# Seven octets in the first chunks' absorb, GpSimd's adds for seven pairs, and octet six's copies on another queue

## The chip, the cores and the metric

The kernel runs on one core of one Trainium2 chip. The metric is the device time of one execution in microseconds (us), as the median of several runs. A profiled execution gives the trace; its times are counted from the start of the span, that is, from the first to the last instruction of the core.

## What is computed

The reference, cut to what matters: linear attention with a feature map of two exponentials, then a Fourier mix of the sequence axis, then a channel product with a relu.

```python
def _attn_ref(q, k, v, w_phi):                    # 8 batches, 8 heads, 576 tokens, 64 wide
    def phi(x):
        proj = np.einsum('bhsd,df->bhsf', x, w_phi)
        proj = proj - np.max(np.abs(proj), axis=-1, keepdims=True)
        return np.concatenate([np.exp(proj), np.exp(-proj)], axis=-1)
    q_p, k_p = (phi(q), phi(k))
    kv = np.einsum('bhsf,bhsd->bhfd', k_p, v)
    z = np.sum(k_p, axis=2)
    num = np.einsum('bhsf,bhfd->bhsd', q_p, kv)
    den = np.einsum('bhsf,bhf->bhs', q_p, z)[..., None] + 1e-06
    return (num / den).astype(np.float32)

def _moe_ref(x, w_r, w_i, w_ch):                  # x: 8 x 576 x 512, the heads side by side
    X = np.fft.rfft(x, axis=1)
    Y = np.zeros_like(X)
    Xr, Xi = (np.real(X[:, :n_modes]), np.imag(X[:, :n_modes]))       # 64 modes
    Yr = np.einsum('bmd,mde->bme', Xr, w_r) - np.einsum('bmd,mde->bme', Xi, w_i)
    Yi = np.einsum('bmd,mde->bme', Xr, w_i) + np.einsum('bmd,mde->bme', Xi, w_r)
    Y[:, :n_modes] = Yr + 1j * Yi
    y = np.fft.irfft(Y, n=S, axis=1)
    u = x + y
    return (u + np.maximum(u @ w_ch, 0.0)).astype(np.float32)
```

## The kernel before

The tokens of a pair of batches (`bp`, 0 to 3) lie in nine chunks (`n`, 0 to 8) of 128 rows: chunk n below 8 holds 128 tokens of one of the two batches, chunk 8 the last 64 of both. The result x of the attention stays in SBUF in bf16, as tile `xs`; `chunk(bp, n)` is its view of one chunk, 128 x 512. The rows of a chunk are in another order than the output wants them, except those of chunk 8: a matmul with the permutation `perm` on the left, in place of the identity `ident_b`, brings them into the stored order.

The first stage (16 units of a group of heads `g` and a pair `bp`) computes the attention and x's first 64 Fourier modes. The mode weights, 64 MB in float32 that pass as bf16 in 1 MB pieces, are loaded by GpSimd's queue (`wload`) throughout the whole run, in the order of the list `order`; tiles of tag `wt` (pool `pw`, eight slots) hold them. The modes are worked off in eight octets `o`. `mix(g, w, ...)` multiplies one piece. Of the list the last eight pieces belong to octets six and seven.

Behind the attention the loop over `mixq` does a `mix`, then some items of the list `todo` (`fill`). In `todo` stand:

- `hold(i)` for each of the 36 chunks: `Channels.turn` transposes the chunk on TensorE (PE) and VectorE (DVE) copies it out as `xT`; `Channels.product` multiplies it by w_ch and ScalarE (ACT) keeps the result in `xw`. Each `hold` first takes a step of the generator `inverse_tables`, which builds the inverse Fourier tables `CI`, `CL`, `CM` on VectorE, with tile `xw` of the last pair as its scratch.
- an `Absorb` for each chunk: `sum_p` adds y's first octets to x, `sum_q` adds y @ w_ch to `xw`, by the identity and by matmuls with `CI` on the left (`back`). Before the change 96 rows, that is octets 0 to 5, take part. VectorE adds x (`keep_x`), ACT keeps `xw` (`keep_w`).

When an octet is complete, its sum `yst` (y) is transposed and multiplied by w_ch, which gives `zst`. `put` copies both by DMA: octets 0 to 5 into the rows of `yall` and `zall` that `Absorb` reads, octets 6 and 7 each four times into `yl`, at the rows that `late` reads.

When the last octet is there, the pairs of chunks in `seq` are finished (class `Last`), 20 items, four of them single chunks. `base(1)` opens a PSUM bank with the permuted `xw` (q), `base(0)` one with the permuted x (p); `late` adds octets 6 and 7 from `yl` with `CL` on the left, q with `late(1)`, p with `late(0)`. For the four chunks with bp = 0 and n below 4 (`early`) `late` adds octet 6 alone and `straight` adds octet 7 straight from `yst` and `zst` with `CM`. `relu` is ACT's relu of q into `rl`; `store` is VectorE's p + rl into `of` (tag `wt`) and the DMA to the output. The banks q come from pool `pst` (four banks), the banks p from `pst2` (two tiles of two banks). The loop at the end prepares q of the next item while it finishes p of the present one:

```python
    for g, s in enumerate(seq):
        t = seq[g + 1] if 0 < g < len(seq) - 1 else None
```

All engines take their instructions in the order in which they are written down (`InOrder`), so an instruction that waits holds up all behind it on its engine. The helper that does this is line 37, which is why most rows of the trace carry L37; they are told apart by their tiles.

Of the kernel before, what the change touches and what calls it, by code (L numbers as in the profile page):

```python
# [20 lines left out]
NG = 4  # L21
# [22 lines left out]
def kernel(  # L44
# [534 lines left out]
    CL = pb.tile([128, 5, 128], BF16, name="CL", bufs=1)  # L579
    perm = CF.rearrange("p c t x m -> p (c t x m)")[:, 512:640]  # L580
# [5 lines left out]
    def inverse_tables():  # L586
# [37 lines left out]
        for dst, m, r, only in ((CI, mode, r, None), (CL, late, r, None), (CM, last, rm, b0)):  # L624
# [17 lines left out]
            if dst is CI:  # L642
                dve.tensor_scalar_mul(out=dst.rearrange("p c s -> p (c s)"), in0=rnd[:, :n],
                                      scalar1=amp)
                yield
                continue
# [9 lines left out]
    class Channels:  # L656
# [4 lines left out]
        def turn(self):  # L661
# [5 lines left out]
            dve.tensor_copy(self.xT, pt)  # L667
# [13 lines left out]
    def back(p, c, bp, table, src, r, stop=True):  # L681

        if c < 8:
            pe.matmul(p, lhsT=table[r, c % 4, :], rhs=src[r, 2 * bp + c // 4, :],
                      start=(src is yall), stop=stop)
        else:
            for i in range(2):
                pe.matmul(p[64 * i:64 * i + 64, :], lhsT=table[r, 4, 0:64],
                          rhs=src[r, 2 * bp + i, :], start=(src is yall), stop=True)

    class Absorb:

        def __init__(self, bp, n):
            self.bp, self.n = bp, n

        def sum_p(self, p):
            self.p = p
            back(p, self.n, self.bp, CI, yall, slice(0, 96))

        def sum_q(self, q):  # L700
            self.q = q
            pe.matmul(q, lhsT=ident_b, rhs=xw[:, self.bp, self.n, :], start=True, stop=False)
            back(q, self.n, self.bp, CI, zall, slice(0, 96))
# [13 lines left out]
        def only_w(self):  # L717
            back(self.q, self.n, self.bp, CI, zall, slice(0, 96))
            self.keep_w()

        def all(self):
            if chunks.index((self.bp, self.n)) % 2:
# [9 lines left out]
    chunks = [(bp, n) for bp in range(NP) for n in range(9)]  # L732
    ch = [Channels(*c) for c in chunks]
    ab = [Absorb(*c) for c in chunks]
    K = len(ch) - 3

    tables = inverse_tables()

    def hold(i):
# [3 lines left out]
        if i < K:  # L743
            ch[i].product()
            return
# [8 lines left out]
    todo += [c.only_x for c in ab[K:]] + [c.only_w for c in ab[K:]] + [c.all for c in ab[:K]]  # L754
# [7 lines left out]
    def put(src, o, dst, copies):  # L762
        if o < 6:
            sp.dma_start(dst[16 * o:16 * o + 16], src)
        else:
            for s in copies:
                r = 32 * s + 16 * (o - 6)
                (sp, pool)[s // 2 if o == 7 else 0].dma_start(yl[r:r + 16], src)


    class Last:

        def __init__(self, *items):
# [3 lines left out]
            self.first = bp == 0 and n < 2  # L777

        def base(self, which):
# [9 lines left out]
            for a, (bp, n) in enumerate(self.items):  # L789
                turned = perm if n < 8 else ident_b  # L790
# [7 lines left out]
        def late(self, which):  # L798
            for a, (bp, n) in enumerate(self.items):
                r = 64 * a + 32 * which  # L800
                back((self.q if which else self.p)[a], n, bp, CL, yl,
                     slice(r, r + 16 if self.early else r + 32), not self.early)
# [11 lines left out]
        def relu(self):  # L814
            self.rl = pb.tile([128, 2, DMODEL], F32, name="rl")
            for a in range(len(self.items)):
                act.activation(self.rl[:, a], self.q[a], ACT.Relu)

# [25 lines left out]
    seq = [Last((0, 0)), Last((0, 1))] + [Last(*x) for x in pairs[0][1:] + pairs[1]]  # L844
    seq += [Last((0, 8), (1, 8))] + [Last(*x) for x in pairs[2]] + [Last((2, 8), (3, 8))]
# [116 lines left out]
```

## Time and profile before

| | us |
|---|---|
| median of 8 runs | 444.65 (443.95 to 445.76) |
| profiled execution | 445.15 |
| its span | 443.2 |
| busy: PE, VectorE, ScalarE, GpSimd | 337.5, 284.2, 279.5, 84.5 |
| mean granted TensorE clock | 0.90 |

A row of the trace gives an instruction's start and duration, the engine, the operation, what it writes and reads with partitions x elements, and how many were merged (x4). In brackets, or behind a bar, stands the engine's idle time before it and what ended it. The end of a matmul is modelled, so two in a row are best told by their starts: 0.217 us from one dense 512-column matmul to the next at full clock. A weight load is PEld, GpSimd is POOL, SyncE's DMA queue is SP.

### The profile page before, as it was taken

Reading aid. Unit: us, or ns where it says so; the run is one execution under the profiler, and the core shown is the slowest. Engines: PE = TensorE matmul, PEld = TensorE weight load, DVE = VectorE, ACT = ScalarE, POOL = GpSimd, SP = SyncE. Lnnn points to the kernel's source line nnn. Section 1 sums busy time; section 2 is a strip of 40 time slices with the busy share of each in tenths; the row PEclk is TensorE's granted clock in tenths of the full one; section 3 lists DMA queues with packets and bytes.
Section 4 is the critical chain, followed back from the end, with each engine's and each line's share of the span. In section 5 each row is a group of like instructions: output and inputs, shape, how many; then the busy total and the mean of one; then the engine's idle time right before and its main releaser. Section 6 shows DMA issues by size and latency. Waiting matters only on the chain.

```text
span 443.2 us, 10464 instructions
## 1 busy us (share of the span) xinstructions
PE 337.5 (76%) x4389; PEld 217.8 (49%) x4433; DVE 284.2 (64%) x561; ACT 279.5 (63%) x488; POOL 84.5 (19%) x126
## 2 busy tenths in 40 slices
PE   3577668677686685785976777876899859999994
PEld 2356547545475573664754655652455424343231
DVE  4667586555865757867668568658744323776685
ACT  4588687666976866867778659433444312665673
POOL 7132122122221211321232021140011110000000
PEclk9969887689988969988889789698899978999998
DMA  8999999999999999999999999999999999993697
GB/s 174 235 211 211 238 212 237 238 212 263 211 213 236 238 236 237 210 238 211 239 220 226 237 212 239 209 213 212 212 224 222 218 219 219 211 220 64 214 383 287
DMA packets 51487, 99.31 MB, mean 224 GB/s; under 512 B 2480, under 2 KB 13616, under 8 KB 51440
## 3 DMA queue, kind: packets, MB, share of 16 engines
q0 software_dynamic: 45280, 86.19, 99.0%
q1 hardware_dynamic: 6160, 12.45, 8.0%
q8 instruction: 34, 0.56, 0.5%
q14 instruction: 13, 0.11, 0.1%
HBM read 163.64 MB, written 9.44 MB: 391 GB/s over the span
## 4 chain that ended last, share of the span: by engine, by line
issue 33%; PE 25%; DMA 13%; ACT 11%; DVE 8%; POOL 8%; POOLq 0%; ACTq 0%; DVEq 0%
DMA wt<-in_moe_w_i_dram 13%; PE pt L37 8%; PE one L37 7%; PE pp L37 5%; PE two L37 5%; POOL wt L37 4%; ACT AB L37 4%; DVE m L37 3%; ACT AQ L37 2%; DVE mk L37 2%; DVE xs L37 1%; ACT XT L37 1%; POOL qb L37 1%; ACT qT L37 1%; POOL kb L37 1%
## 5 line engine op out<-in xcount | busy, mean ns | idle before, releaser
L37 ACT ACTIVATE AB<-two 128x1024 bf16<-128x1024 f32 x64 | 62.1, 1028 | 12.0 <-DVE mk L37 8.6
L37 ACT ACTIVATE AQ<-two 128x1024 bf16<-128x1024 f32 x64 | 62.7, 1047 | 3.5 <-PE two L37 3.4
L37 ACT CAST xw<-pt 128x512 bf16<-128x512 f32 x50 | 29.4, 587 | 40.8 <-PE pt L37 40.7
L37 DVE TENSOR_REDUCE mk<-two 128x8 f32<-128x1024 f32 x32 | 38.9, 1218 | 14.5 <-PE two L37 14.5
L37 DVE TENSOR_REDUCE m<-two 128x8 f32<-128x1024 f32 x32 | 39.2, 1224 | 12.8 <-PE two L37 12.6
L37 DVE RECIPROCAL rd<-one 128x6 f32<-128x6 f32 x48 | 9.4, 195 | 55.9 <-PE one L37 55.8
L37 DVE TENSOR_TENSOR va<-vn,ee 128x1152 bf16<-128x1152 f32 x32 | 41.9, 1353 | 0.0
L37 PE MATMUL pt<-wchb,xT 128*128 128x512 bf16 x128 | 36.4, 399 | 6.0 <-DVE xT L37 4.5
L37 ACT COPY kT<-one 128x512 bf16<-128x512 bf16 (+1 forms) x32 | 19.3, 640 | 31.0 <-PE one L37 30.9
L37 PEld LDWEIGHTS <-xs 128*128 128x128 bf16 x624 | 31.9, 103 | 12.9 <-issue 7.0
L37 PEld LDWEIGHTS <-minus 96*128 96x128 bf16 x288 | 28.0, 116 | 17.7 <-issue 12.5
L37 PE MATMUL two<-w2blk,qT 128*128 128x256 bf16 x128 | 20.9, 289 | 19.1 <-ACT AB L37 9.2
L37 POOL DMA_DIRECT2D wt<-in_moe_w_r_dram x30 | 22.3, 744 | 68.5 <-PE one L37 34.8
L37 POOL DMA_DIRECT2D wt<-in_moe_w_i_dram x28 | 20.9, 746 | 74.3 <-PE one L37 39.8
L37 PE MATMUL two<-mT,minus 96*128 96x128 bf16 x256 | 30.8, 255 | 3.7 <-issue 2.5
L37 PEld LDWEIGHTS <-qT 128*128 128x128 bf16 x144 | 14.3, 102 | 36.6 <-issue 33.9
L37 PE MATMUL one<-wt,XT 128*32 128x512 bf16 x304 | 26.6, 436 | 5.9 <-DVE XT L37 2.7
L37 PE MATMUL one<-kvz,AQ 128*128 128x65 bf16 x512 | 29.5, 217 | 0.0
L37 PEld LDWEIGHTS <-XT 128*32 128x32 bf16 x512 | 14.5, 149 | 27.9 <-issue 13.7
L37 DVE TENSOR_TENSOR xs<-one,rd 128x384 bf16<-128x384 f32 x48 | 26.7, 557 | 1.6
L37 PEld LDWEIGHTS <-AQ 128*128 128x128 bf16 x512 | 26.5, 115 | 1.4 <-issue 0.4
L37 PE MATMUL two<-w2blk,kT 128*128 128x256 bf16 x128 | 21.1, 293 | 7.8 <-ACT AB L37 7.8
(131 smaller groups left out, 687.4 us busy)
## 6 DMA issues: line engine op xcount, KB each, us to landing
wt<-in_moe_w_r_dram POOLq DMA_DIRECT2D x30, 1024.0 KB, 21.8
wt<-in_moe_w_i_dram POOLq DMA_DIRECT2D x28, 1024.0 KB, 22.4
vn<-in_v_dram POOLq DMA_DIRECT2D x15, 576.0 KB, 17.9
out_dram<-of SPq DMA_DIRECT2D x16, 512.0 KB, 3.1
kb<-in_k_dram POOLq DMA_DIRECT2D x16, 288.0 KB, 15.4
qb<-in_q_dram POOLq DMA_DIRECT2D x16, 288.0 KB, 15.5
xs<-in_moe_w_i_dram POOLq DMA_DIRECT2D x2, 1024.0 KB, 24.2
yacc<-in_moe_w_r_dram POOLq DMA_DIRECT2D x1, 1024.0 KB, 9.6
```

Source lines behind the costliest of these rows:

```text
L37: ins = f(*args, **kwargs)
```

## The change

- `CD` is a second inverse table, `CI` with its columns in stored order, in a step of its own in `inverse_tables`. Ten chunks are `stored` and stand first in `chunks`. For these `turn` writes `xT` in stored order and `back_x` transposes it back and ACT copies it over the chunk, so that x and `xw` of these chunks are in stored order from there on.
- `Absorb` of the early chunks takes 112 rows, that is octet 6 too, and stands last (`full`); `put` copies octet 6 into `yall` and `zall` as well. `late` of early chunks falls away.
- The ten stored chunks (five pairs) and the two pairs of chunk 8 are `later`: `base(0)` does nothing for them, `late(0)` opens the bank, and GpSimd adds x to the relu's output (a tile `rx` of tag `wt`).
- `seq` takes the two pairs of chunk 8 at other places, and `ahead` says for each item which q to prepare in its step. A `later` item is prepared two or three steps before its store.
- `put` issues octet 6's copies to `yl` from GpSimd's queue, octet 7's from SP and, for the last, ACT.

```diff
--- before.py
+++ after.py
@@ -577,6 +577,8 @@
     yl = pw.tile([128, B_, DMODEL], BF16, name="yl", tag="wt")
     CI = pb.tile([128, 5, 128], BF16, name="CI", bufs=1)
     CL = pb.tile([128, 5, 128], BF16, name="CL", bufs=1)
+    CD = pb.tile([128, 4, 128], BF16, name="CD", bufs=1)
+    stored = [(1, 0), (1, 1), (1, 4), (1, 5), (2, 0), (2, 1), (2, 6), (2, 7), (3, 4), (3, 5)]
     perm = CF.rearrange("p c t x m -> p (c t x m)")[:, 512:640]
     dve.tensor_copy(perm.rearrange("k (p a) -> k a p", a=2),
                     ident_b.rearrange("k (a p) -> k a p", a=2))
@@ -643,6 +645,11 @@
                 dve.tensor_scalar_mul(out=dst.rearrange("p c s -> p (c s)"), in0=rnd[:, :n],
                                       scalar1=amp)
                 yield
+                for a in range(2):
+                    dve.tensor_copy(
+                        CD.rearrange("k c (p a) -> k a c p", a=2)[:, a],
+                        CI[:, 0:4].rearrange("k c (a p) -> k a c p", a=2)[:, a])
+                yield
                 continue
             for c in range(4):
                 dve.tensor_scalar_mul(
@@ -664,7 +671,17 @@
             for g in range(NG):
                 pe.transpose(pt[:, g, :], x[:, g, :], ident_b)
             self.xT = pb.tile([128, 4, 128], BF16, name="xT")
-            dve.tensor_copy(self.xT, pt)
+            if (self.bp, self.n) in stored:
+                dve.tensor_copy(self.xT.rearrange("p g (k a) -> p g a k", a=2),
+                                pt.rearrange("p g (a k) -> p g a k", a=2))
+            else:
+                dve.tensor_copy(self.xT, pt)
+
+        def back_x(self):
+            px = bank([128, 4, 128], BF16)
+            for g in range(NG):
+                pe.transpose(px[:, g, :], self.xT[:, g, :], ident_b)
+            act.copy(chunk(self.bp, self.n), px)
 
         def product(self):
             pf = bank()
@@ -678,29 +695,32 @@
                 pe.matmul(pf, lhsT=self.xT[:, g, :], rhs=wchb[:, g, :],
                           start=(g == 0), stop=False)
 
-    def back(p, c, bp, table, src, r, stop=True):
+    def back(p, c, bp, table, src, r, stop=True, start=False):
 
         if c < 8:
             pe.matmul(p, lhsT=table[r, c % 4, :], rhs=src[r, 2 * bp + c // 4, :],
-                      start=(src is yall), stop=stop)
+                      start=start or src is yall, stop=stop)
         else:
             for i in range(2):
                 pe.matmul(p[64 * i:64 * i + 64, :], lhsT=table[r, 4, 0:64],
-                          rhs=src[r, 2 * bp + i, :], start=(src is yall), stop=True)
+                          rhs=src[r, 2 * bp + i, :], start=start or src is yall, stop=stop)
 
     class Absorb:
 
         def __init__(self, bp, n):
             self.bp, self.n = bp, n
+            self.table = CD if (bp, n) in stored else CI
+            self.early = bp == 0 and n < 4
+            self.rows = slice(0, 112 if self.early else 96)
 
         def sum_p(self, p):
             self.p = p
-            back(p, self.n, self.bp, CI, yall, slice(0, 96))
+            back(p, self.n, self.bp, self.table, yall, self.rows)
 
         def sum_q(self, q):
             self.q = q
             pe.matmul(q, lhsT=ident_b, rhs=xw[:, self.bp, self.n, :], start=True, stop=False)
-            back(q, self.n, self.bp, CI, zall, slice(0, 96))
+            back(q, self.n, self.bp, self.table, zall, self.rows)
 
         def keep_x(self):
             x = chunk(self.bp, self.n)
@@ -715,11 +735,11 @@
             self.keep_x()
 
         def only_w(self):
-            back(self.q, self.n, self.bp, CI, zall, slice(0, 96))
+            back(self.q, self.n, self.bp, self.table, zall, self.rows)
             self.keep_w()
 
         def all(self):
-            if chunks.index((self.bp, self.n)) % 2:
+            if full.index(self) % 2:
                 p, q = bank(), bank()
             else:
                 t = banks()
@@ -730,9 +750,11 @@
             self.keep_w()
 
     chunks = [(bp, n) for bp in range(NP) for n in range(9)]
+    chunks.sort(key=lambda c: c not in stored)
     ch = [Channels(*c) for c in chunks]
     ab = [Absorb(*c) for c in chunks]
     K = len(ch) - 3
+    full = sorted(ab[:K], key=lambda c: c.early)
 
     tables = inverse_tables()
 
@@ -742,6 +764,8 @@
             ch[i + 1].turn()
         if i < K:
             ch[i].product()
+            if chunks[i] in stored:
+                ch[i].back_x()
             return
         if i == K:
             t = banks()
@@ -751,7 +775,7 @@
         ch[i].hold(ab[i].q)
 
     todo = [ch[0].turn] + [lambda i=i: hold(i) for i in range(len(ch))]
-    todo += [c.only_x for c in ab[K:]] + [c.only_w for c in ab[K:]] + [c.all for c in ab[:K]]
+    todo += [c.only_x for c in ab[K:]] + [c.only_w for c in ab[K:]] + [c.all for c in full]
     A = 3 * 3 + K
 
     def fill(n):
@@ -760,12 +784,12 @@
                 todo.pop(0)()
 
     def put(src, o, dst, copies):
-        if o < 6:
+        if o < 7:
             sp.dma_start(dst[16 * o:16 * o + 16], src)
-        else:
+        if o > 5:
             for s in copies:
                 r = 32 * s + 16 * (o - 6)
-                (sp, pool)[s // 2 if o == 7 else 0].dma_start(yl[r:r + 16], src)
+                (pool if o == 6 else act if s == 3 else sp).dma_start(yl[r:r + 16], src)
 
 
     class Last:
@@ -775,6 +799,7 @@
             bp, n = items[0]
             self.early = bp == 0 and n < 4
             self.first = bp == 0 and n < 2
+            self.later = n == 8 or items[0] in stored
 
         def base(self, which):
             if self.first:
@@ -787,7 +812,9 @@
                 self.pp = banks()
                 self.p = [self.pp[:, a] for a in range(2)]
             for a, (bp, n) in enumerate(self.items):
-                turned = perm if n < 8 else ident_b
+                turned = ident_b if self.later else perm
+                if self.later and not which:
+                    continue
                 if which:
                     pe.matmul(self.q[a], lhsT=turned, rhs=xw[:, bp, n, :],
                               start=True, stop=False)
@@ -796,10 +823,12 @@
                               rhs=chunk(bp, n), start=True, stop=False)
 
         def late(self, which):
+            if self.early:
+                return
             for a, (bp, n) in enumerate(self.items):
                 r = 64 * a + 32 * which
                 back((self.q if which else self.p)[a], n, bp, CL, yl,
-                     slice(r, r + 16 if self.early else r + 32), not self.early)
+                     slice(r, r + 32), True, self.later and not which)
 
         def straight(self, which):
             if self.early:
@@ -812,9 +841,16 @@
             act.copy(self.rl[:, 0], self.p[0])
 
         def relu(self):
-            self.rl = pb.tile([128, 2, DMODEL], F32, name="rl")
+            if self.later:
+                self.rl = pw.tile([128, 2, DMODEL], F32, name="rx", tag="wt")
+            else:
+                self.rl = pb.tile([128, 2, DMODEL], F32, name="rl")
             for a in range(len(self.items)):
                 act.activation(self.rl[:, a], self.q[a], ACT.Relu)
+            if self.later:
+                for a, c in enumerate(self.items):
+                    x = self.rl[:, a].rearrange("p (g e) -> p g e", g=4)
+                    pool.tensor_tensor(out=x, in0=x, in1=chunk(*c), op=ALU.add)
 
         def store(self):
             (bp, n), w = self.items[0], len(self.items)
@@ -841,9 +877,10 @@
                 o.rearrange("p a e -> p (a e)") if w > 1 else o)
 
     pairs = [[((bp, n), (bp, n + 1)) for n in (0, 2, 4, 6)] for bp in range(NP)]
-    seq = [Last((0, 0)), Last((0, 1))] + [Last(*x) for x in pairs[0][1:] + pairs[1]]
-    seq += [Last((0, 8), (1, 8))] + [Last(*x) for x in pairs[2]] + [Last((2, 8), (3, 8))]
+    seq = [Last((0, 0)), Last((0, 1))] + [Last(*x) for x in pairs[0][1:] + pairs[1] + pairs[2]]
     seq += [Last(*x) for x in pairs[3][:3]] + [Last((3, 6)), Last((3, 7))]
+    seq.insert(11, Last((0, 8), (1, 8)))
+    seq.insert(15, Last((2, 8), (3, 8)))
     H = DMODEL // 2
     while mixq:
         key = mixq.pop(0)
@@ -911,23 +948,30 @@
     seq[1].straight(0)
     seq[1].straight(1)
     seq[1].relu()
+    ahead = {1: [2], 2: [3], 3: [4, 5], 4: [7], 5: [6], 6: [9], 7: [8], 8: [11], 9: [10], 10: [13],
+             11: [12], 12: [15], 13: [14], 14: [17], 15: [16], 16: [18], 17: [19], 18: []}
     for g, s in enumerate(seq):
-        t = seq[g + 1] if 0 < g < len(seq) - 1 else None
-        if t and g > 1:
-            t.base(1)
-        if g > 1:
+        ts = [seq[i] for i in ahead.get(g, [])]
+        if ts and g not in (1, 3):
+            ts[0].base(1)
+        if g > 1 and g != 3:
             s.base(0)
-            if g == 2:
-                s.late(0)
-                s.straight(0)
-        if t:
+        if g == 2:
+            s.straight(0)
+            seq[4].base(1)
+            seq[3].base(0)
+        for t in ts[:1]:
             t.late(1)
         if g > 2:
             s.late(0)
-        if t:
+        for t in ts[:1]:
             t.straight(1)
             t.relu()
         s.store()
+        for t in ts[1:]:
+            t.base(1)
+            t.late(1)
+            t.relu()
     pb_cm.__exit__(None, None, None)
     pw_cm.__exit__(None, None, None)
```

## The prediction

> **What bounds the kernel now.** I read the page first (PE busy 76% of the span, DMA busy in nearly every slice up to 400 us), then busy time by stretches, then the instructions in order of time, then the groups after 411 us. All times are us from the span's start.
>
> ```profile
> 362.00:366.00 4.00, 3.12 (x19) 1.41 (x19) 1.04 (x3) 0.37 (x1) 0.74 (x1) 0.50 1.13 213
> 394.00:406.40 12.40, 12.19 (x67) 4.48 (x66) 9.71 (x15) 8.10 (x15) 0.00 (x0) 1.00 0.71 126
> 406.40:411.30 4.90, 4.84 (x33) 2.14 (x34) 2.16 (x5) 1.59 (x4) 1.10 (x2) 1.00 0.22 54
> 411.30:416.20 4.90, 4.47 (x24) 1.32 (x23) 1.93 (x3) 2.79 (x6) 0.00 (x0) 1.00 0.65 171
> 416.20:438.30 22.10, 20.77 (x124) 6.29 (x122) 19.56 (x17) 16.22 (x30) 0.00 (x0) 1.00 0.89 359
> ```
>
> The columns are length, then busy time of PE, weight load, DVE, ACT and POOL, the granted clock, DMA share and GB/s. Up to 362 the weight stream leads (213 GB/s, DMA share over 1). From 362 to the last `mix` at 406.4 PE has hardly a gap: it works off the 33 `Absorb`s, and no wait for a weight is left. From 416 to 438 three engines run level: PE, VectorE and the output at 359 GB/s, which in 420 to 422 reached 406 GB/s, so 512 KB in 1.29 us. POOL does nothing there.
>
> ```profile
> 307.56 1.89 PE L37 MATMUL pt<-wchb,xT 128*128 128x512 bf16 x4 [2.13 <-DVE xT L37]
> 350.66 0.66 PE L37 MATMUL pt<-wt,XT 128*32 128x512 bf16 x8 [1.45 <-DMA wt<-in_moe_w_i_dram]
> 362.16 1.08 PE L37 MATMUL pt<-wt,XT 128*32 128x512 bf16 x8 [3.21 <-DMA wt<-in_moe_w_i_dram]
> 405.43 0.38 PE L37 MATMUL pp<-yl,CL 16*128 16x512 bf16 x1
> 406.38 0.66 PE L37 MATMUL pt<-wt,XT 128*32 128x512 bf16 x8
> 413.68 1.23 DVE L37 TENSOR_TENSOR of<-pp,rl 128x1024 f32<-128x1024 f32 x1 [1.32 <-PE pp L37]
> 416.19 6.39 DVE L37 TENSOR_TENSOR of<-pp,rl 128x1024 f32<-128x1024 f32 x5 [1.28 <-PE pp L37]
> 437.55 0.69 DVE L37 TENSOR_TENSOR ofr<-pp,rl 128x512 f32<-128x512 f32 x1 [0.24 <-ACT rl L37]
> ```
>
> In brackets stands the wait before the row. PE waits 1.45, then 0.92 (at 356.01), then 3.21 us for weights: 5.6 us of slack before its backlog begins. After 3.21 us idle, and after 2.13, the next matmuls take twice as long (1.08 against 0.66, 1.89 against 1.03); after 1.45 they don't. The last `zst` half is ready at 410.02 (call it Z). The final sums on VectorE run to 438.24, which is Z+28.22; the span ends 4.96 us later.
>
> ```profile
> L37 DVE TENSOR_TENSOR of<-pp,rl 128x1024 f32<-128x1024 f32 x16 | 19.5, 1225 | 4.8 <-PE pp L37 4.1
> L37 PE MATMUL pp<-xs,CF 128*128 128x512 bf16 x30 | 9.1, 379 | 0.5 <-DVE of L37 0.4
> ```
>
> Of VectorE's 4.8 us of waiting between pairs PE causes 4.1. Five `of` in 6.39 us are 1.28 each, the pace to reach.
>
> **Part 1: early chunks absorb octet six.** Their eight `late` matmuls go. Four stand between 405.12 and 406.38 (base, late, base, late, each 0.31 because the row tile changes): 1.26 us. Two bases alone are 2 x 0.217 (a dense matmul's spacing) and 0.1 for the switch to the mix, so the last `mix` starts 0.73 earlier. It has room: its weight was issued at 370.37 and took 34.5, so landed at 404.9, and without part 3's copies in its way earlier still. What follows from the mix to Z is a latency chain (yst, turn, product, zst) that stays: **Z' = 409.29**. The longer absorb (112 rows for 96) costs nothing on PE, as 96 and 128 rows both show 0.38; the four absorbs come last, after 401, and octet six's zst copies of before landed at about 399.
>
> **Part 2: seven pairs take x from GpSimd.** It removes 14 `base(0)` matmuls, 14 x 0.217 = 3.0 us of PE. A step of 1.30 (two bases of 0.43, lates 0.43) becomes 0.87 at every second pair, so PE falls to 1.08 a pair on average and VectorE's 1.28 would set the pace. It adds three costs.
>
> (a) *POOL's adds.* Fourteen 128x512 adds that no row of before shows. The nearest rows:
>
> ```profile
> masks.py:199 POOL TENSOR_SCALAR_AFFINE_SELECT xs<-xs 128x128 f32<-128x128 f32 x1 | 0.3, 292 | 0.1
> masks.py:197 POOL MEMSET xs<- 128x128 f32 x1 | 0.2, 198 | 0.0
> L946 POOL MEMSET const-float32-1.0<- 128x1 f32 x1 | 0.1, 99 | 0.0
> ```
>
> Fixed cost 0.10; writing 0.77 ns an element ((198-99)/127); reading one input 0.73 more ((292-198)/128). One input at 512 elements would be 0.87 us, my lower end; a second input that costs as much as all of the first (1.5 ns) gives 1.64, my upper end. I take one more read stream, 0.10 + 512 x 2.23 ns = 1.24 us, the sum nearest to what the add does; with 0.05 between instructions 1.29. (The Trainium skill, GPSIMD Engine Reference, sections 3.1 and 4.1, advises against elementwise adds here, about twice VectorE's time: 4497 ns for 2048 elements. That would be an estimated 1.12 us, and by it the tail below would end about 0.4 us sooner.)
>
> (b) *The new order*, followed from Z'. seq[2] no longer waits for two late groups (0.32 and 0.42 in the trace): its store starts at Z'+2.7 instead of Z+3.66. seq[3] needs the octet-seven copies, issued at Z' with 3.4 to land (the SP row's median; POOL's second copy was issued 0.54 later and landed at Z+4.27): late at Z'+3.7, two relus of 0.55, store at Z'+5.1 to 6.35 (before: Z+6.17). seq[4]: `base(1)` of seq[7] is queued on PE ahead of `base(0)` of seq[4], and needs the PSUM banks that seq[4]'s relus free at Z'+6.16; then 0.43 + 0.43 + 0.43 and 0.4 of latency: store at Z'+7.7 to 8.95, a new gap of 1.3 us on VectorE. seq[5]: its relus are third in line on ACT (first half done Z'+6.7), so the adds run 6.75 to 9.3 and the store follows at 9.3.
>
> (c) From there POOL is the longest queue: 6.75 + 14 x 1.29 = 24.8, then `of` of seq[17] (0.05 + 1.24) and two single stores (0.73 each): **Z'+27.55**. VectorE alone, 1.28 x 13 + 1.46 after seq[4], would end at 27.1, so POOL costs 0.45. ACT (1.09 a pair) is hidden under both. The output, 1.29 a pair at 406 GB/s against 1.28, ends up some 0.2 later behind VectorE than now.
>
> Tail: 409.29 + 27.55 = 436.84 against 438.24, -1.4; with the output's 0.2, **-1.2 us**.
>
> (d) *Before 365.* Ten `back_x`: 4 transposes each, 0.23 us of PE (the spacing from turn to product), so 2.3 us; ten more ACT copies of 0.58 (ACT is under half busy). Ten strided xT copies and two for CD on VectorE, bounded by the dense row (0.42, no extra) and the permuting CF row:
>
> ```profile
> L37 DVE COPY xT<-pt 128x512 bf16<-128x512 bf16 x36 | 15.1, 420 | 13.3 <-PE pt L37 13.3
> L37 DVE COPY CF<-ident_b 128x128 bf16<-128x128 bf16 x1 | 0.3, 313 | 0.0
> ```
>
> A permuting copy pays (0.313-0.16)/128 = 1.2 ns an element, so up to 0.77 for 512: 3.5 us for ten, and some 0.9 for CD. VectorE is 90% busy there (10.81 of 12 us in 299 to 311) and PE waits for it, so PE falls behind by 2 to 6 us; I take 4. The 5.6 us of slack cover it; without that cover it would be paid in full. The wait at 362 then shrinks from 3.21 to 3.21 + 2.37 - 4 = 1.6 us, between the 1.45 that left the clock alone and the 2.13 that halved it. The half clock costs 2.2 us in 362 to 367 (rows 1.08, 0.72, 1.89, 0.63, 1.59 against 0.66, 0.58, 1.04, 0.38, 1.03). So this term lies between 0 and **-2.2**, and PE's backlog carries it to the end; I take -0.8. If PE falls behind by over 8 us the sign turns. (The Trainium skill, TensorE: Matmul & The Clock Gate, Part 1, puts the throttle at an idle window of about 3.4 us. The 2.13 row speaks against so sharp a bound; by the page the whole 2.2 would be won.)
>
> **Part 3: copies.** Octet six's four yl copies move from SP to POOL's queue, behind the last weights: POOL has nothing queued but the adds, and they are needed only at Z'+3.5. Two yall and zall copies come to SP. Net 0.25 MB less beside the weights (1.2 us at 213 GB/s), which hides behind PE's backlog. ACT issues one octet-seven copy; the 0.55 us of a SP issue fits before its relu at Z'+0.9. Nothing.
>
> **Sum.** Against the profiled execution (445.15, span 443.2, 1.95 around it): -1.2 - 0.8 = -2.0. The median of the runs shown is 444.65, 0.5 lower; taking the difference from it: **442.65 us**.
>
> **Rivals.** *POOL becomes the bound, and it is slower than before.* Each 0.1 us on an add is 14 x 0.1 = 1.4 us at the end. The tail's gain is gone at an add of (28.95 - 0.2 - 2.75 - 6.75)/14 - 0.05 = 1.32; with part (d) at 1.38. At 1.47 the time is 444.65 + 1.2 = 445.9 with (d), 446.7 without; at 1.64 448.2. For it: the second input shares whatever reads the first, and the seven pairs leave it only 2 x 1.28 per turn. Against: the memset and select rows. *It does not do what it says*: the gaps at seq[3] and seq[4] and slots of `wt` (rx joins `of` and yl in eight, and an `of` is free only 4.5 us after it starts) eat the tail's gain, and the clock dips as before: 444.4. *The holds overrun*: PE falls behind by over 8 us: up to 446. *Everything fits*: adds at 0.87 (-0.5) and no dip (-1.4 more): 440.7.
>
> **Numbers.** About 0.2% (0.9 us) is what a measurement of this kernel tells from no change. The forecast, with its better case, 0.62, all faster; no effect 0.12; POOL-bound 0.20 and holds overrun 0.06, slower. Range 440.7 (everything fits) to 446.6 (an add of 1.47 without the clock's help), leaving out the slower POOL adds.
>
> **What would show it.** POOL rows in the tail: fourteen adds near 1.24 us, the store of a `later` pair ending its wait on POOL. Gaps on VectorE before the stores of seq[3] and seq[4] only. The wait before the mix near 362 under 2 us and its matmuls at 0.66. Last mix about 0.7 (2 with the clock) earlier than 406.38. If the adds are over 1.33 us, or the wait for the weight near 362 is still 3 us, I am wrong in that term.

## The result, and the profile after

The changed kernel takes **443.02 us** (median of 11 runs, 441.81 to 443.88), against 444.68 us (31 runs, 443.78 to 445.76) for the kernel before in the same session. The ratio is 0.9962, 95% interval 0.9951 to 0.9972: 1.66 us less, where 2.0 were forecast (442.65).

The profiled execution took 442.19 us (span 440.3), the one of before 445.15 (443.2). The two differ by 2.96, the medians by 1.66: the profile of after caught one of its quicker executions and that of before one slower than its median. The traces serve for the order of events; what a part is worth is read from medians.

First the timeline of PE and the chain of waits of after, around the points of the prediction.

```profile
362.10 0.66 PE L37 MATMUL pt<-wt,XT 128*32 128x512 bf16 x8
...
403.76 0.66 PE L37 MATMUL pt<-wt,XT 128*32 128x512 bf16 x8
```

```profile
367.94 0.28 issue
368.22 35.49 DMA wt<-in_moe_w_i_dram
403.76 0.68 PE pt L37 x8
```

At 362 PE no longer waits, and its matmuls take 0.66 where they took 1.08: PE has fallen behind by the whole 5.6 us of slack, not by 4. The last `mix` starts at 403.76, 2.62 earlier than before (406.38). The second fence says why not earlier still: the chain that ended last goes from that `mix` to the transfer of its weight, issued at 368.22 and landed at 403.71. Before, the weight had landed at 404.9 and PE came 1.5 later; now PE and the weight arrive together.

That the weight itself lands 1.2 earlier goes with the copies: part 3 takes four from beside it and part 1 brings two. POOL did issue the load 2.15 earlier (368.22 for 370.37: a `mix` frees a slot of `wt`, and there was no half clock before it), but over the runs below the landing does not follow the issue. It follows the number of small copies of octet six that SP's queue moves beside the last weights: with none (e9, e5) the last weight lands at 402.6 and 403.0, with two (after and the eight kernels that keep its copies) at 403.2 to 404.5, with four (e1, before) at 404.6 and 404.9, with six (e2) at 405.9. The two ends of this row, from the DMA view of e9, where the load was issued at 370.21, and of e2, where it was issued at 368.02 (the last number is the time from issue to landing):

```profile
wt<-in_moe_w_i_dram POOLq DMA_DIRECT2D x1, 1024.0 KB, 32.4
```

```profile
wt<-in_moe_w_i_dram POOLq DMA_DIRECT2D x1, 1024.0 KB, 37.9
```

Next VectorE in the tail of after, with `zst` as its first row.

```profile
406.96 0.42 DVE L37 CAST zst<-pt 128x256 bf16<-128x256 f32 x1 [1.07 <-PE pt L37]
...
412.71 1.23 DVE L37 TENSOR_TENSOR of<-pp,rl 128x1024 f32<-128x1024 f32 x1 [1.41 <-ACT rl L37]
415.00 1.22 DVE L37 TENSOR_TENSOR of<-pp,rl 128x1024 f32<-128x1024 f32 x1 [1.07 <-PE pp L37]
416.60 1.22 DVE L37 TENSOR_TENSOR of<-pp,rx 128x1024 f32<-128x1024 f32 x1 [0.37 <-POOL rx L37]
417.74 1.21 DVE L37 TENSOR_TENSOR of<-pp,rl 128x1024 f32<-128x1024 f32 x1
...
431.67 1.22 DVE L37 TENSOR_TENSOR of<-pp,rx 128x1024 f32<-128x1024 f32 x1 [0.28 <-DMA out_dram<-of]
...
434.15 0.69 DVE L37 TENSOR_TENSOR ofr<-pp,rl 128x512 f32<-128x512 f32 x1 [0.67 <-issue]
```

Z' is 406.96 + 0.42 = 407.38. The gaps stand where they were forecast: before the store of seq[3] (1.41), of seq[4] (1.07), of seq[5] (0.37, on POOL). Then stores start 1.13 to 1.22 us apart where nothing holds them (416.60, 417.74), not 1.28; with three short waits (0.27 and 0.39 on PE, 0.28 on a tile) it is 1.26 on average up to 431.67, against 1.38 for the pairs of before from 416.19 on, their waits included. The 0.28 at 431.67 is new in kind: VectorE waits for a transfer to free a tile of `wt`. VectorE ends at 434.84, Z'+27.46. POOL's group in the tail, and then its timeline:

```profile
L37 POOL TENSOR_TENSOR rx<-rx,xs 128x512 f32<-128x512 f32 x14 | 15.8, 1158 | 26.9 <-ACT rx L37 26.9
```

```profile
414.29 11.24 POOL L37 TENSOR_TENSOR rx<-rx,xs 128x512 f32<-128x512 f32 x10 [26.27 <-ACT rx L37]
425.76 2.27 POOL L37 TENSOR_TENSOR rx<-rx,xs 128x512 f32<-128x512 f32 x2 [0.24 <-ACT rx L37]
```

Ten adds in 11.24 are 1.12 us each. From 425 on it is POOL that waits for ACT: it is not the bound. Last the output: stretches of after (columns as in the prediction; the last three are clock, DMA share and GB/s), then two lines of the DMA view from 420 to 436, of after and below it of before (the queue's packets, MB and share of the 16 engines; the transfers issued, KB each, median us to landing).

```profile
362.00:366.00 4.00, 3.18 (x28) 1.85 (x29) 1.80 (x5) 1.33 (x3) 0.74 (x1) 1.00 1.12 221
...
420.00:424.00 4.00, 4.00 (x26) 1.14 (x25) 3.73 (x5) 3.56 (x7) 4.00 (x4) 1.00 1.01 409
424.00:428.00 4.00, 4.00 (x26) 1.04 (x24) 3.60 (x4) 3.07 (x7) 3.76 (x4) 1.00 1.00 393
428.00:432.00 4.00, 3.24 (x19) 0.89 (x18) 3.71 (x4) 2.93 (x6) 2.31 (x3) 1.00 1.02 400
432.00:436.00 4.00, 1.25 (x3) 0.19 (x2) 2.18 (x3) 0.07 (x1) 0.00 (x0) 0.57 1.02 398
```

```profile
q1 hardware_dynamic: 2005, 6.38, 100.8%
...
out_dram<-of SPq DMA_DIRECT2D x11, 512.0 KB, 4.8
```

```profile
q1 hardware_dynamic: 1891, 5.95, 92.3%
...
out_dram<-of SPq DMA_DIRECT2D x12, 512.0 KB, 3.0
```

From 420 to 436 the sixteen DMA engines are full, at 393 to 409 GB/s; before they were at 92%. At 409 GB/s a 512 KB store takes 1.28 us, at 393 GB/s 1.33, and VectorE now makes one every 1.26, at times every 1.14. So stores queue: from issue to landing goes from 3.0 to 4.8 us, and the span ends 5.46 us behind VectorE, not 4.96. From 420 on the output has taken VectorE's place as what sets the end.

### The profile page after: what moved, and what is told of

It is laid out like the page before. It is cut to its first block, busy times and chain, and to the rows that moved or that the text cites. A ratio compares the mean times of both kernels' runs of the same rounds, so it can differ in the third digit from the quotient of the medians.

```text
span 440.3 us, 10540 instructions
## 1 busy us (share of the span) xinstructions
PE 336.0 (76%) x4407; PEld 218.6 (50%) x4451; DVE 287.0 (65%) x563; ACT 283.0 (64%) x498; POOL 101.3 (23%) x142
## 4 chain that ended last, share of the span: by engine, by line
issue 28%; PE 25%; DMA 14%; ACT 12%; DVE 12%; POOL 7%; POOLq 0%; ACTq 0%; DVEq 0%
DMA wt<-in_moe_w_i_dram 12%; PE pt L37 12%; PE one L37 7%; PE two L37 5%; ACT AB L37 4%; POOL wt L37 4%; DVE m L37 3%; ACT AQ L37 3%; DVE mk L37 2%; DVE xw L37 2%; ACT qT L37 1%; ACT XT L37 1%; DMA out_dram<-of 1%; ACT xw L37 1%; PE pp L37 1%
## 5 line engine op out<-in xcount | busy, mean ns | idle before, releaser
L37 POOL DMA_DIRECT2D kb<-in_k_dram x16 | 11.5, 718 | 80.8 <-PE one L37 80.0
L37 PEld LDWEIGHTS <-xT 128*128 128x128 bf16 x184 | 16.6, 102 | 21.3 <-DVE xT L37 6.7
```

The lines of the kernel that those rows point to most:

```text
L37: ins = f(*args, **kwargs)
```

## The experiments

**Theory:** the gain is the earlier last `mix`, which needs PE (part 1) and the weight (part 3) together; behind it the output sets the end, so part 2 brings little. **Rivals:** part 2's lighter tail brings it; POOL's adds hold the tail back; or the work that part 2 adds to the holds pays for itself, because PE falls behind instead of idling into a lower clock. The ratio of each kernel is to the kernel before on the same chip (medians 444.5 to 444.8 us); medians are of 4 to 12 executions. The last three columns are of one profiled execution, with that execution's own Z. They are good to some tenths only: in e9 and e1 VectorE ends as far behind Z as in before (28.28 and 28.23), and their last column differs by 0.7.

| kernel | median us | ratio [95%] | last `mix` | VectorE's end - Z | span's end - Z |
|---|---|---|---|---|---|
| before | 444.68 | 1 | 406.38 | 28.22 | 33.2 |
| after | 443.02 | 0.9962 [0.9951, 0.9972] | 403.76 | 27.46 | 32.9 |
| e11: parts 1 and 3 | 443.39 | 0.9965 [0.9952, 0.9977] | 405.51 | 27.47 | 32.5 |
| e9: part 3 | 444.23 | 0.9989 [0.9977, 1.0001] | 406.23 | 28.28 | 32.6 |
| e5: parts 2 and 3 | 443.85 | 0.9994 [0.9975, 1.0013] | 404.89 | 28.02 | 33.5 |
| e2: parts 1 and 2 | 444.78 | 1.0008 [0.9995, 1.0020] | 406.01 | 27.60 | 33.0 |
| e3: after, no adds | 442.79 | 0.9958 [0.9943, 0.9973] | 404.02 | 27.41 | 33.2 |
| e4: after, no back_x | 442.57 | 0.9951 [0.9937, 0.9965] | 404.86 | 26.73 | 32.5 |
| e1: before, extra work in holds | 443.88 | 0.9986 [0.9972, 1.0001] | 404.92 | 28.23 | 33.3 |
| e6: after, half the output | 439.58 | 0.9887 [0.9866, 0.9909] | 403.89 | 26.70 | 30.3 |
| e10: eight early chunks | 443.23 | 0.9962 [0.9947, 0.9978] | 405.08 | 27.05 | 32.9 |
| e12: e11 and four adds | 443.19 | 0.9966 [0.9953, 0.9979] | 404.70 | 27.29 | 32.7 |
| e14: e12, eight early | 442.52 | 0.9954 [0.9938, 0.9970] | 404.33 | 27.12 | 32.4 |
| e15: e14, other order | 442.84 | 0.9956 [0.9938, 0.9974] | 404.03 | 27.39 | 32.6 |

### Which part brings it

**e11: part 2 undone, parts 1 and 3 kept.** `stored` is empty, no pair is `later`, CD is not built, and the order is one ahead again. The places of the chunk-8 pairs and the banks that steps 2 and 3 open ahead stay as in after:

```diff
-    stored = [(1, 0), (1, 1), ...]
+    stored = []
...
-            self.later = n == 8 or items[0] in stored
+            self.later = False
...
-    ahead = {1: [2], 2: [3], 3: [4, 5], ...}
+    ahead = {g: [g + 1] for g in range(1, 19)}
```

> The changed kernel with its second part undone: no chunk is stored, no CD, no back_x, no add on GpSimd; parts one (seven octets in the early chunks) and three (copies) stay, and each item is prepared one step ahead as before. Theory (output transfers bound the last 15 us, so taking matmuls from the tail brings little, and the hold work it costs is as dear as it brings): the last mix near 405.5, VectorE's end at Z+27.4 and with holes that the transfers follow, time 442.8 to 443.6, that is within 0.6 us of the changed kernel. By the prediction's sum (tail part with its clock gain 1.2 of 2.0 us) it would lose 1 to 1.3 us against the changed kernel: 444.0 to 444.3.

Measured 443.39: the same as after within the intervals. The largest part of the diff is worth 0.37 us by the medians, which these runs can't tell from nothing. VectorE's stores in its timeline:

```profile
414.53 9.02 DVE L37 TENSOR_TENSOR of<-pp,rl 128x1024 f32<-128x1024 f32 x7 [1.46 <-ACT rl L37]
```

Seven stores in 9.02 are 1.29 each: without GpSimd's adds the stores keep the old pace, which is near PE's (six matmuls of 0.217 a pair) and near the output's. From Z to the end of the span it takes 32.5 us, after 32.9: no gain of the quicker pace of part 2 can be seen there.

**e3: after without the fourteen adds** (x is left out of those seven pairs).

```diff
-                    pool.tensor_tensor(out=x, in0=x, in1=chunk(*c), op=ALU.add)
+                    pass
```

> The changed kernel without the fourteen adds on GpSimd (x is left out of the sums of seven pairs). Theory (POOL is not the bound; from the seventh pair on the output transfers are, at 1.29 us a pair): the store of seq[5] starts up to 1 us earlier, the end moves by 0 to -0.8 us. Rival (POOL is the longest queue, as the prediction's sum had it): -1 us or more.

442.79 against 443.02, well inside each other's spread: no cost of POOL's adds can be seen, and the rival that POOL is the bound falls.

**e9: part 3 alone, on the kernel before.**

```diff
-                (sp, pool)[s // 2 if o == 7 else 0].dma_start(yl[r:r + 16], src)
+                (pool if o == 6 else act if s == 3 else sp).dma_start(yl[r:r + 16], src)
```

> The kernel of before with the copies of the change alone: octet six's four yl copies on GpSimd's queue behind the weights, octet seven's on SP and ACT. Theory (the copies matter only where PE's backlog no longer hides the last weight): the last weight lands about 2 us earlier than 404.9, the last mix stays at 406.4, and the time falls by 0.2 to 0.7 us only, from the yl copy that lands 0.7 us earlier. Rival (the copies are most of the gain whatever else is done): -1.2 us or more.

444.23, or 0.6 us less by the medians, with an interval that just touches no change. The last weight lands at 402.6, 2.3 earlier than before, but in the trace no row from 398 to the last `mix` waits for a weight: PE is the later of the two, and the `mix` stays at 406.23. So what the 0.6 us would come from, if they are real, is not shown.

**e2: part 3 undone in after** (the same line the other way round).

> The changed kernel with the yl copies of octets six and seven on the queues of before (octet six on SP beside the weights; the new yall and zall copies stay). Theory: the last mix of the changed kernel waits for its weight, so what lies beside the weights now counts: 0.5 MB more at 213 GB/s is 2.4 us later landing (about 406), and the time rises by 1.5 to 2.5 us. By the prediction (the copies hide behind PE's backlog) it stays the same within 0.3 us.

444.78: **the whole gain is gone**, 1.76 us. The timeline of PE of this run:

```profile
401.10 0.67 PE L37 MATMUL pt<-wt,XT 128*32 128x512 bf16 x8 [0.84 <-DMA wt<-in_moe_w_r_dram]
406.01 0.66 PE L37 MATMUL pt<-wt,XT 128*32 128x512 bf16 x8 [1.50 <-DMA wt<-in_moe_w_i_dram]
```

PE is early enough, as in after, but waits 0.84 and 1.50 for the last weights. The last one takes 37.9 us from issue to landing (34.5 in before, 35.5 in after): here part 1's two copies and the four of before stand beside it. The `mix` is back at 406.

**e5: part 1 undone in after** (the early chunks absorb 96 rows, and octet six comes late).

```diff
-            self.rows = slice(0, 112 if self.early else 96)
+            self.rows = slice(0, 96)
...
-        if o < 7:
+        if o < 6:
...
-            if self.early:
-                return
...
```

> The changed kernel without the early chunks' seventh octet: they absorb six, octet six reaches them by late from yl as before, and the two yall and zall copies fall away. The prediction priced this part at 0.73 us before the last mix and 0.75 us behind it. Theory: the last mix about 0.7 us later, the store of seq[2] 0.7 us later from Z, and since the transfers are the bound behind that, the time rises by 0.7 to 1.5 us against the changed kernel.

443.85, or 0.83 us longer than after, as expected. (Two of its twelve executions took 446.5 and 447.8; with them its ratio would make it 1.4.)

Together, by the medians: part 1 is worth 0.84 us beside part 3 alone (e9 to e11) and 0.83 in after; part 3 0.6 alone and 1.8 in after; part 2 0.4 both in after and beside part 3 alone, which these runs can't tell from nothing (by the ratios 0.1 less and 0.2 more time). Part 1 alone and part 2 alone were not run. The `mix` waits for the later of PE and the weight, so moving one helps only until the other is late. That is the theory, and it holds for what parts 1 and 3 do in after; the rivals of the tail and of POOL are refuted.

### The work in the holds

**e1: before, with sixteen useless rewrites of x** (four transposes and an ACT copy each; the values don't change).

```diff
+    def again(c):
+        px = bank([128, 4, 128], BF16)
+        for g in range(NG):
+            pe.transpose(px[:, g, :], c.xT[:, g, :], ident_b)
+        act.copy(chunk(c.bp, c.n), px)
...
+            if i < 16:
+                again(ch[i])
```

> The kernel of before with useless work: sixteen of the holds transpose x back and copy it over itself (64 transposes on PE, 16 copies on ACT of 0.58 us). Theory (the hold work of the change pays for itself, since it uses up PE's slack before 362 us and so keeps the clock up): PE falls behind by 4 to 6 us, the wait of 3.21 us before the mix near 362 is under 1.5 us, its matmuls take 0.66 and not 1.08, the last mix starts 1.0 to 1.5 us earlier than 406.38 (its weight landed at 404.9, which caps it), and the kernel gets FASTER than before by 0.8 to 1.5 us, although it only has more to do. Rival (the change gains only in the tail, the clock plays no part): same as before or slower by up to 1 us.

443.88: 0.9 us less by the medians, 0.6 by the ratio, whose interval just includes no change. PE's row at the place of the 3.21 us wait:

```profile
361.11 0.66 PE L37 MATMUL pt<-wt,XT 128*32 128x512 bf16 x8 [1.77 <-DMA wt<-in_moe_w_i_dram]
```

64 transposes and 16 copies more don't cost a measurable time: PE's slack hides them, as the prediction held for `back_x`. Whether they gain is not settled: the interval includes no change. In this one execution the last `mix` starts at 404.92, 0.3 behind the landing of its weight (issued at 368.90, 35.7 us).

**e4: after without `back_x`** and with plain xT copies (x of the ten stored chunks keeps its old row order).

```diff
-            if (self.bp, self.n) in stored:
+            if False:
...
-            if chunks[i] in stored:
-                ch[i].back_x()
```

> The changed kernel without back_x and with plain xT copies, so that x of the ten stored chunks keeps its old order (this part of the computation is left out; all later instructions stay). Theory: PE falls behind by only about 1 us, the wait before the mix near 362 is back at 2.5 us or more with matmuls at half clock behind it, the last mix is at 405.0 to 406 instead of 403.8, and the time is 1.2 to 2.0 us LONGER than that of the changed kernel (about 444.2 to 445.0), with less work. Rival: shorter by up to 0.5 us or the same.

442.57: the theory of useful work wanted it longer, and it is 0.45 shorter, with overlapping intervals. PE waits 2.87 us at 361.83 and runs some 3 us at half clock behind it; the last weight is issued at 369.60, the `mix` starts at 404.86, 1.1 later than in after, and this profiled execution (442.76) is 0.6 longer than that of after (442.19). The medians go the other way. So by five and eleven runs the work in the holds brings nothing to after that can be seen; if anything it costs some tenths. **The theory that it pays for itself is not borne out there**; the trace shows a way by which it could, and for the kernel before e1 leaves it open.

### What sets the end

**e6: after with half of each output tile's columns stored**, but for the two pairs of chunk 8, which are stored whole. VectorE, PE and POOL do the same work.

```diff
-                        ap=[[9 * DMODEL, 64], [4 * DMODEL, 2], [1, w * DMODEL]]),
+                        ap=[[9 * DMODEL, 64], [4 * DMODEL, 2], [1, w * DMODEL // 2]]),
...
```

> The changed kernel that stores only the first half of each finished tile's columns (the other half of the output is left out). Theory (the output is the bound of the last 15 us: landings grow from 3.0 to 5.0 us, VectorE waits for a free tile before the store of seq[17]): the landings stay near 2.5 to 3 us, no wait on an output transfer, the time falls by 1.5 to 2.5 us. Rival (VectorE, PE or GpSimd sets the end): VectorE ends at the same distance from Z (27.3 to 27.5 us) and only the last landing is shorter, -0.5 to -1.0 us.

439.58, 3.4 us less than after: more than expected. In the traces 2.6 of it lie behind Z: VectorE ends 0.8 earlier, and the span's end follows it 1.9 closer, to which the halved last transfer itself adds. Its stretch that answers to the one at 400 GB/s above:

```profile
428.00:432.00 4.00, 3.24 (x20) 0.89 (x18) 4.00 (x4) 2.89 (x6) 2.47 (x3) 1.00 0.70 265
```

DMA share 0.70 for 1.02, 2.4 us to landing (the 256 KB stores from 420 to 436) for 4.8, no wait for a free tile, VectorE at Z+26.70 and the span's end 3.58 behind it. The output was the bound of the later part of after's tail: with about half of it, Z to the span's end is 30.3 us for 32.9.

### Other versions

**e10: after with eight early chunks** instead of four, for which a second table `CN` is built and later items change places.

```diff
-            self.early = bp == 0 and n < 4
+            self.early = bp == 0 and n < 8
...
+    CN = pb.tile([128, 4, 128], BF16, name="CN", bufs=1)
...
```

> The changed kernel taken further: eight early chunks and not four (both batches of the first pair absorb octet six and get octet seven straight from yst and zst, by a second table CN), so that four pairs need no copy through yl; the order of the later items is moved by one. Theory (behind Z the output transfers bound the end, and the holes before the stores of seq[3] to seq[5], 2.9 us of VectorE, are holes in the transfers too): the stores of seq[2] to seq[5] run without a gap over 0.7 us, the transfers are dense 3 to 4 us earlier, and the time falls by 1.5 to 3 us against the changed kernel (440.0 to 441.5). Rival (the end is set by GpSimd or PE further back): within 0.7 us of the changed kernel.

443.23, no gain. The gap moves, by VectorE's timeline, to seq[5] (1.68 us before its store at 417.58): a relu for a later item stands ahead on ACT.

**e12: e11 with GpSimd's adds for the two chunk-8 pairs alone**, which need no other row order, so no CD and no `back_x`.

```diff
-            self.later = False
+            self.later = n == 8
...
```

> As the kernel with the second part undone, but the two pairs of chunk 8, which need no hold work since they lie in stored order anyway, still get x from GpSimd. Theory: 0.3 to 0.6 us less than without GpSimd, as the two gaps around these pairs (0.34 and 0.41 us each in the kernel of before) close: 442.3 to 443.2.

443.19, like e11 and after. **e14** adds the eight early chunks of e10 to e12:

> As the kernel with GpSimd for the two pairs of chunk 8 alone, and eight early chunks with the second table CN, each item one step ahead, so that nothing queued on ScalarE stands between the early pairs and the first that waits for the copies. Theory (what counts behind Z is when the transfers become dense): stores of VectorE without a gap from the store of seq[2] on (Z+2.7), its end at Z+25 to Z+25.5, the time 440.3 to 441.5, less than both kernels. Rival: the transfers at 1.29 us a pair or the PE at 1.30 leave it within 0.7 us of the changed kernel.

442.52, the shortest of the versions that compute the same, though its interval (0.9938 to 0.9970) overlaps that of after, and the expected 440.3 to 441.5 is missed. In its timeline the gaps at seq[3] to seq[5] are 0.50 or less each, and one has come back later:

```profile
423.44 1.23 DVE L37 TENSOR_TENSOR of<-pp,rl 128x1024 f32<-128x1024 f32 x1 [1.23 <-PE pp L37]
```

**e15: e14 with the chunk-8 pairs one place later and seq[10]'s base(0) and late(0) ahead on PE.**

```diff
-    seq.insert(11, Last((0, 8), (1, 8)))
-    seq.insert(15, Last((2, 8), (3, 8)))
+    seq.insert(12, Last((0, 8), (1, 8)))
+    seq.insert(16, Last((2, 8), (3, 8)))
...
+        if g == 10:
+            s.base(0)
+            s.late(0)
```

> The order of e14 with two edits: the chunk-8 pairs stand one place later in the sequence, so that their adds on GpSimd have one more step, and in step 10 base(0) and late(0) of seq[10] are queued ahead of base(1) and late(1) of the next item. In e14 VectorE had a gap of 1.23 us before the store of seq[10] (its base(0) was queued on PE behind a base(1) that waited for q banks) and one of 0.36 behind it, waiting for GpSimd. Theory (VectorE's gaps are worth what they measure as long as the output keeps up): the first gap shrinks to some 0.4 and the second goes, VectorE ends 1.0 to 1.2 us earlier than in e14, and the time is 0.5 to 1.0 below e14, 441.5 to 442.0. Rival (the output transfers are the bound by then, as in the changed kernel): VectorE's gap comes back as a wait for out_dram, and the time stays within 0.4 of e14's 442.52.

442.84, no gain, as the rival had it, but not by the rival's wait: the gap moves on by one store (0.99 us on PE before the one at 424.57).

All thirteen kernels of the table with a full output need 32.4 to 33.5 us from Z to the span's end. That does not make the output a floor that nothing can lower. Stretches of 4 us from the tails of after (8 to 12 us behind its Z), of e11 (8 to 12, then 16 to 20) and of e14 (16 to 20), columns as above:

```profile
415.38:419.38 4.00, 3.80 (x23) 1.04 (x22) 3.63 (x4) 3.62 (x8) 4.00 (x5) 1.00 0.67 275
```

```profile
417.14:421.14 4.00, 4.00 (x26) 1.32 (x25) 3.78 (x4) 3.35 (x7) 0.00 (x0) 1.00 0.99 402
425.14:429.14 4.00, 4.00 (x28) 1.24 (x24) 3.42 (x3) 3.11 (x6) 0.00 (x0) 1.00 0.89 355
```

```profile
423.95:427.95 4.00, 4.00 (x27) 1.35 (x26) 3.51 (x4) 3.02 (x6) 2.50 (x3) 1.00 0.69 276
```

Behind the gaps at seq[3] to seq[5] the output of after runs at a share of 0.67, where e11, without the gap at seq[4], already has 0.99. Later e11 falls to 0.89, while after stays full: what part 2 wins there it had lost at the start. e14 fills the start and has a hole of 0.69 behind its later gap. No version kept the output full from Z+8 to the end, and what that would bring was not measured.

## Why the prediction was right, point by point

The time was right (442.65 forecast, 443.02 measured, inside the range) and so was the side. The sum was made up differently from what the runs show.

- **Part 1**, -0.73: right. Undoing it cost 0.83 (e5); adding it to part 3 brought 0.84, and the `mix` came 0.72 earlier (406.23 in e9, 405.51 in e11).
- **The adds on POOL**, 1.24 us taken, 1.12 in a row and 1.16 on average measured. The ends 0.87 and 1.64 held it, and the estimate was a tenth too high. By the prediction's own split the second input would take an estimated 0.5 ns an element, less than the 0.73 of the first; no run parts the two. The estimate from the Trainium skill, GPSIMD Engine Reference, section 3.1 (1.12 us), agrees with the row. The page's advice against such adds does not decide here either way: leaving them out moves the time by 0.2 us, less than the runs can tell.
- **The new order**: right in kind. Stores of seq[3] and seq[4] were forecast at Z'+5.1 and Z'+7.7 and came at 5.33 and 7.62; VectorE's end at Z'+27.55 came at 27.46.
- **The pace**: mis-sized. The 1.28 us that the prediction read as VectorE's pace was not VectorE's own; it starts stores 1.14 apart when PE and POOL let it. The error hid behind the next one.
- **The output**, +0.2: mis-sized, measured +0.5, and more than a size. The prediction had the output's own pace, 1.29 a pair, beside the pace it forecast for VectorE, and took them for level. Once the output is full, any store faster than that only waits in the queue. The tail term of part 2 (-0.5 beyond part 1) is -0.3 by the traces from Z to the span's end (33.2 to 32.9), and e11 has 32.5 without part 2: no gain can be seen.
- **The holds**, -0.8: the chain up to the clock was right (PE behind, no wait at 362, clock 1.00 for 0.50) but its last step, "PE's backlog carries it to the end", holds in the trace alone (the last `mix` and Z' come 2.6 earlier) and not in the medians: the kernel without this work and with the dip (e4) is not slower. PE fell behind by all of the 5.6 us, the edge of its cover, not by 4. The length of the wait, by which the prediction chose the size, is also not what the half clock goes by (see the last section). What the term is worth stays open: e4 speaks for 0, e1 for something between 0 and -0.9.
- **Part 3**, "Nothing": **the step that failed.** Undoing it costs 1.76 us (e2). The prediction gave the room itself: the weight lands at 404.9, "without part 3's copies in its way earlier still", and part 1 brings the `mix` to 405.65. With the clock's -0.8 the `mix` stands at 404.85, before the weight. From that point the copies in the weight's way are on the path; they were priced for the kernel before, whose PE was late enough to hide them. With them in place the weight lands at 405.9 and the `mix` waits 1.50 for it.

That the sum came out at -2.0 against -1.66 is therefore partly luck: -1.3 were booked for part 2, which brought 0.4 by the medians or nothing, and nothing for part 3, without which nothing would have come. Of the rivals, POOL as the bound is refuted by e3, and the overrun of the holds by the trace of after (5.6 us behind, not over 8). "It does not do what it says" is true for part 2: the gaps do hold back the output, as that rival had it, and the full output behind them leaves nothing to win back; the clock did not dip, and slots of `wt` cost 0.28 us.

## What to carry to other kernels

When several terms of a sum shorten the way to one instruction, list everything it waits for with its arrival time, and price each edit against the state that the other edits leave: here PE and a weight were 1.5 us apart, and moving one without the other gave about half of the gain or less (e5, e9) or none of it (e2). Before a stage is made faster, compare its pace with that of the transfers that leave it; here the output takes 1.28 us a pair or more, so faster stores behind a gap won nothing; what is left to try is keeping it full from an earlier time. The pace of a group of merged rows belongs to the slowest engine behind it, not to the one that shows it.

## What the runs showed of the hardware

The granted clock does not follow the length of the wait alone. Mixes near 362 after a wait of 3.21, 3.29 and 2.20 us (before, e9, e11) took 1.08, at half clock at once; after 3.23, 3.13 and 2.87 us (e12, e14, e4) they took 0.66 to 0.67, and the half clock came 2 us later, in the middle of work. The timeline of e12:

```profile
361.73 0.67 PE L37 MATMUL pt<-wt,XT 128*32 128x512 bf16 x8 [3.23 <-DMA wt<-in_moe_w_i_dram]
...
363.72 1.89 PE L37 MATMUL pt<-wchb,yT 128*128 128x256 bf16 x8 [0.19 <-ACT yT L37]
```

It was seen behind 1.77 us too (e1: mean clock 0.68 from 362 to 366) and not behind 1.81 (e15: 1.00). The clock's record in the traces says what the moment goes by. In all fourteen, every stretch at one clock, from one change to the next, lasts a multiple of 3.41 us (6.83 at half clock in before, from 361.09; 3.41 in e12, from 363.58). So the clock changes only at marks of this spacing, and these lie differently to the program in each execution. What goes with the change is PE's busy time between two marks, by the profile's modelled ends. A stretch of e1, behind which came half clock, and one of e15, behind which the clock stayed full:

```profile
360.01:363.42 3.41, 1.55 (x15) 0.73 (x15) 1.05 (x3) 0.37 (x1) 0.74 (x1) 1.00 1.12 223
```

```profile
361.20:364.61 3.41, 1.94 (x19) 1.09 (x19) 1.05 (x3) 0.37 (x1) 0.74 (x1) 1.00 1.13 225
```

Of the 1350 such stretches at full clock in the fourteen traces, all 174 with PE busy for less than 1.55 us were followed by half clock, and of the 1080 with 1.85 or more only one was; in between both occur. So a wait of 2 us can be enough, and where it falls between the marks decides. The Trainium skill, TensorE: Matmul & The Clock Gate, Part 1, speaks of an idle window of about 3.4 us, free-running; the spacing agrees, but here a window with up to about half of it busy was followed by half clock.

A copy from PSUM that changes the order of 512 bf16 columns by a step of two costs VectorE about 0.72 us against 0.42 for the plain one: 36 xT copies, ten of them permuting, took 18.1 us in after and 15.1 before. The permuting row of before (0.77) had bounded it from above.
